# Attention and mixture of experts on one core: the first round's rows gathered in parts, two groups in quarter rows, one weight load in 4 KB pieces, fewer filler matmuls

## Chip, core and metric

The kernel runs on one core of one Trainium2 chip. The metric is device time in microseconds (us). The time before is the median of three runs; every time in this part comes from those runs or from the hardware profiler's record of one more execution.

Engines are named as in the profile: PE is TensorE (PEld its weight loads), DVE is VectorE, ACT is ScalarE, POOL is GpSimd, SP is SyncE, which here only starts DMA transfers. `L247` is line 247 of the kernel before. Where rows of the changed kernel are shown, the line numbers are those of the changed file.

## What is computed

```
attn = softmax(q k^T / 8) v                  # 8 batches x 8 heads, chunks of 64 tokens, head size 64
x    = attn as 4608 rows of 512              # fp32
logits = x @ w_gate                          # 8 experts
expert_idx = argmax(logits); gate_w = softmax(logits)[expert_idx]
for e in range(8):
    tok = rows whose expert is e; if more than capacity (80): keep the 80 with the largest gate_w
    h = relu(x[tok] @ w1[e])                 # 512 -> 1024
    out[tok] = gate_w[tok] * (h @ w2[e])     # 1024 -> 512; all other rows are zero
```

All weights and activations of the experts are fp32. One expert's `w1` or `w2` is 2 MB.

## The kernel before

**Up to the selection.** Attention runs over 36 tiles of 128 rows; its output rows go to a DRAM scratch tensor `xs`, from which rows are gathered later. Gating and the search for each expert's cut-off run beside it. Then the tokens that can be kept are packed: one-hot matrices `pk`, made on DVE in five compares (L849) and on ACT in three pairs of Abs and Relu (L859, L860), are multiplied on PE (L1100) into 128 candidates, and their keys stand in `kc` (L1112).

**Selection.** Every expert has 96 slots. For each expert PE turns its key column into a row (L1139), DVE counts how many candidates are larger (`rank`, L1120) and compares the rank with the slot numbers (`select`, L1126), which gives a 0/1 matrix `sel`. `place` (L166) multiplies `sel` with the candidates' row numbers and gate values. Slots are handled in groups of 32: expert e owns groups 3e to 3e+2, and round r works on groups 4r to 4r+3, so there are six rounds. Round 0 holds three groups of expert 0 and one of expert 1. `place` writes round 0 into `pl0` and rounds 1 to 5 into `pl1`; a DVE sum (L170) turns these into row numbers `gi0` and `gi1`.

**Gathers.** POOL starts an indirect DMA (L204) that fetches the 128 rows of a round from `xs` into `xg`, one row of 2 KB per partition. For rounds 0 and 1 PE turns `xg` by four transposes into PSUM (L217) and ACT copies the result to `xT` (L219), round 0 in two halves. Rounds 2 to 5 are fetched instead as four quarter gathers of 512 B per partition (L228, the addresses `giq` come from two DVE operations behind a spreading matmul L1163), so that DVE can turn them in blocks of 32 (L237).

**Experts.** `layer1(r, f)` (L247) handles two groups (j = 0, 1) with 16 PE products each, every product two passes in the trace; ACT applies ReLU (L252), DVE turns the result (L254). `layer2` (L264) follows one round later, DVE scales (L269), POOL scatters (L273). PE's order is: layer1 of round 0 and 1, layer2 of round 0, layer1 of round 2, layer2 of round 1, and so on.

**What sets the order.** The program is written out by hand: every engine runs its instructions in the order of the code, and waits are put in from the data that the instructions share. Weights come on SP's queue in the order of the code (`part`, called from `ahead`); expert 3's `w1` is held back by a POOL memset into its first column that stands behind the second gather (L1202), experts 4's `w1` and 3's `w2` by DVE copies that read the second gather's rows (L1204). `keep_warm(n)` (L871) puts n matmuls of 256 columns, whose result nobody reads, into PE's order. `RUN` makes a weight load move 16 KB at a time.

## Time and profile before

| what | value |
|---|---|
| median of 3 runs | 233.46 us (232.95 to 233.56) |
| the profiled execution, its own time | 233.38 us |
| its span, first to last instruction | 231.6 us |
| PE busy in the span | 217.0 us (94%) |
| DVE, ACT, POOL busy | 133.5, 73.0, 66.7 us |
| DMA | 84.81 MB, mean 366 GB/s |

The profiled execution's time is the span and what lies around it. "Busy" adds up the times in which an engine has an instruction running; matmuls are pipelined, so that a busy PE may also be doing fillers.

### The profile page before, as it was taken

How to read it: one execution, taken by the hardware profiler on the slowest of the kernel's cores; microseconds unless marked ns; L12 is line 12 of the kernel's file. 1: busy time of each engine (PE TensorE's matmuls, PEld its weight loads, DVE VectorE, ACT ScalarE, POOL GpSimd, SP SyncE). 2: the span in 40 equal slices, each digit the busy share in tenths (PEclk: the TensorE clock that was granted, in tenths of full speed). 3: DMA queues.
4: the chain of work that ended last, by engine and by line, in shares of the span. 5: the costliest groups of instructions: out<-in, count | busy, mean ns of one | idle time of the engine just before them, and what ended most of it. 6: DMA issues, size and time to landing. Idle time of an engine off the chain costs nothing. (4 is left out here: it accounts for less than half of the span.)

```text
span 231.6 us, 8390 instructions
## 1 busy us (share of the span) xinstructions
PE 217.0 (94%) x3604; PEld 143.0 (62%) x3604; DVE 133.5 (58%) x422; ACT 73.0 (32%) x159; POOL 66.7 (29%) x142
## 2 busy tenths in 40 slices
PE   7878999999898999999999999999999999999970
PEld 5667787877777787878776876653534436354220
DVE  6678687878779799878878866213231321302110
ACT  2124433333535635566585501210110201111000
POOL 8001203030303019292624427107033060411101
PEclk9999999999999999999999999999999999999998
DMA  6999999999999999998999977999999999998011
GB/s 214 362 409 396 413 410 417 421 421 420 416 419 408 372 406 402 410 413 284 379 420 420 417 298 279 333 423 427 431 405 428 441 397 425 444 420 362 5 44 38
DMA packets 16681, 84.81 MB, mean 366 GB/s; under 512 B 2752, under 2 KB 2880, under 8 KB 12288
## 3 DMA queue, kind: packets, MB, share of 16 engines
q1 hardware_dynamic: 12848, 71.84, 76.6%
q0 software_dynamic: 3648, 12.32, 13.7%
q8 instruction: 30, 0.49, 0.8%
q10 hardware_dynamic: 144, 0.07, 0.2%
q14 instruction: 11, 0.09, 0.1%
HBM read 64.03 MB, written 20.45 MB: 365 GB/s over the span
## 5 line engine op out<-in xcount | busy, mean ns | idle before, releaser
L247 PE MATMUL hc<-w,xtc 128*32 128x256 f32 x768 | 42.6, 379 | 0.3 <-ACT xtc L219 0.3
L264 PE MATMUL yc<-w,htc 128*32 128x512 f32 x384 | 42.1, 592 | 0.0
L419 PE MATMUL s<-kz,qv 128*64 128x128 f32 x544 | 37.2, 279 | 0.5 <-DMA qv<-in_qv 0.5
L247 PEld LDWEIGHTS hc<-w,xtc 128*32 128x32 f32 x768 | 24.8, 110 | 18.4 <-issue 2.4
L455 ACT ACTIVATE pT<-pt 128x512 f32<-128x512 f32 x36 | 21.4, 594 | 36.7 <-PE pt L453 36.5
L419 PEld LDWEIGHTS s<-kz,qv 128*64 128x64 f32 x544 | 29.0, 136 | 6.3 <-issue 6.1
L435 DVE TENSOR_REDUCE mx<-s 128x8 f32<-128x512 f32 (+1 forms) x37 | 24.9, 673 | 11.4 <-PE s L419 11.2
L264 PEld LDWEIGHTS yc<-w,htc 128*32 128x32 f32 x384 | 12.5, 110 | 26.6 <-issue 25.7
L478 PEld LDWEIGHTS o<-qv,pT 64*64 64x64 f32 x1120 | 19.8, 134 | 13.1 <-issue 9.6
L252 ACT ACTIVATE hsc<-hc 128x512 f32<-128x512 f32 x12 | 7.2, 598 | 62.6 <-PE hc L247 62.6
L478 PE MATMUL o<-qv,pT 64*64 64x65 f32 x1120 | 24.9, 224 | 2.1 <-DMA qv<-in_qv 1.2
L254 DVE STREAM_TRANSPOSE htc<-hsc 128x512 f32<-128x512 f32 x12 | 8.5, 711 | 31.1 <-ACT hsc L252 31.1
L437 DVE TENSOR_TENSOR sm<-s,mx 128x512 f32<-128x512 f32 (+1 forms) x37 | 24.7, 667 | 0.1
L497 DVE TENSOR_TENSOR x<-o,rc 128x512 f32<-128x512 f32 x35 | 24.1, 689 | 0.8
L453 PE MATMUL pt<-ct,sm 128*128 128x128 f32 x144 | 23.5, 285 | 0.2
L269 DVE TENSOR_SCALAR ysc<-yc,gatec 128x512 f32<-128x512 f32 x6 | 4.5, 750 | 33.1 <-PE yc L264 24.6
L513 PE MATMUL px<-ct,x 128*128 128x128 f32 x136 | 20.5, 273 | 0.0
L514 ACT COPY xT<-px 128x512 f32<-128x512 f32 x32 | 18.6, 580 | 0.0
L591 POOL TENSOR_TENSOR comp<-comp,ct 128x32 bf16<-128x32 bf16 x18 | 3.9, 234 | 50.3 <-DVE rc L492 40.8
L228 POOL DMA_INDIRECT xqc<-xs,giq x16 | 16.0, 1003 | 6.1 <-issue 4.8
L453 PEld LDWEIGHTS pt<-ct,sm 128*128 128x128 f32 x144 | 15.2, 140 | 2.8 <-DVE sm L437 0.4
L513 PEld LDWEIGHTS px<-ct,x 128*128 128x128 f32 x136 | 15.9, 141 | 0.8 <-issue 0.8
(223 smaller groups left out, 228.2 us busy)
## 6 DMA issues: line engine op xcount, KB each, us to landing
w<-in_w SPq DMA_DIRECT2D x12, 2048.0 KB, 22.6
qv<-in_qv SPq DMA_DIRECT2D x14, 1032.0 KB, 11.1
kz<-in_kh SPq DMA_DIRECT2D x34, 256.0 KB, 10.2
xs<-x POOLq DMA_DIRECT2D x8, 1024.0 KB, 11.7
w<-in_w SPq DMA_DIRECT2D x8, 1024.0 KB, 9.6
out<-zero SPq DMA_DIRECT2D x8, 1024.0 KB, 26.7
qv<-in_qv SPq DMA_DIRECT2D x2, 520.0 KB, 9.2
qv<-in_qv SPq DMA_DIRECT2D x2, 516.0 KB, 9.7
```

The source lines that it names most:

```text
L228: nc.gpsimd.indirect_dma_start(out=t[:, P * g:P * g + P], out_offset=None, in_=xs.rearrange("r (c d) -> (r c) d", c=4), in_offset=bass.Ind ...
L247: nc.tensor.matmul(h[32 * c:32 * c + 32, j, :], lhsT=xT[r][:, g, b, :], rhs=w[:, b, 256 * c:256 * c + 256], start=(b == 0), stop=(b == 3), ...
L264: nc.tensor.matmul(y[o:o + 32, :], lhsT=hT[r, g // 2][:, g % 2, c, :], rhs=getw(groups[r][g])[1][:, c, :], start=(c == 0), stop=(c == 7), ...
L419: nc.tensor.matmul(o, lhsT=a, rhs=b, start=True, stop=True)
L435: nc.vector.tensor_reduce(m8, s8, axis=AX.X, op=ALU.max)
L437: d['sub'] = lambda: nc.vector.tensor_tensor(d8, s8, to, op=ALU.subtract)
L453: nc.tensor.transpose(pt[:, pr, :], sv[:, pr, :], ident)
L455: nc.scalar.activation(pT, pt, AF.Exp, scale=0.125)
L478: nc.tensor.matmul(po[h][64 * u:64 * u + 64, 65 * pr:65 * pr + 65], lhsT=d['pT'][64 * h:64 * h + 64, pr, 64 * u:64 * u + 64], rhs=TT[T, r] ...
L497: nc.vector.tensor_tensor(x8, pov[..., 0:64], to, op=ALU.mult)
L513: nc.tensor.transpose(pm[:, pr, :], t['x'][:, r, P * pr:P * pr + P], ident)
L514: copy(t['xT'][:, :, P * r:P * r + P], pm)
```

## The change

It has six parts.

1. **Round 0 is gathered in parts.** The first 64 rows (groups 0 and 1, both of expert 0) are placed, summed and gathered (`xga`) as soon as expert 0's rank and `sel` are there. Groups 2 and 3 are fetched as two quarter gathers (`xgh`), whose addresses `gih` come from eight more `place` matmuls, a DVE sum and a DVE multiply-add.
2. **Turning.** `xga` is turned by four PE transposes of 64 columns that stand behind the `place` matmuls of rounds 1 to 5, ahead of the matmuls for the flag and the quarter addresses; `xgh` by one DVE transpose ahead of `targets`. Round 1's PE transposes move from between the two halves of round 0's layer 1 to the middle of its second half.
3. **Selects.** `sel` of experts 2, 3 and 5 is made on ACT (Abs, Relu) instead of DVE.
4. **Fillers.** `keep_warm` has 1 instead of 2 (three times), 2 instead of 4, 14 instead of 18, 4 instead of 6, none instead of 8.
5. **Expert 3's `w1`** moves 4 KB at a time instead of 16 KB, and waits for the last transpose of `xga` instead of the POOL memset.
6. The buffers of `xg` are 3 instead of 4; `xga` and `xgh` are set to zero early in the program.

```diff
+    xga = mp.tile([P, DM], F32, name="xga")
+    xta = mp.tile([P, 4, 64], F32, name="xta")
+    xgh = mp.tile([P, 2 * P], F32, name="xgh")
+    xth = mp.tile([P, 2, 4, 32], F32, name="xth")
...
-        def layer1(r, f):
+        def layer1(r, f, between=None):
             h = pp.tile([P, 2, 256], F32, name=f"h{tag}{r}_{f}", tag="h", bufs=4)
             for j in range(2):
+                if j and between:
+                    between()
...
-                            h[32 * c:32 * c + 32, j, :], lhsT=xT[r][:, g, b, :],
+                            h[32 * c:32 * c + 32, j, :],
+                            lhsT=xT[r][f][:, j, b, :] if extra and r == 0 else xT[r][:, g, b, :],
...
-        for r in range(NQ if extra else 2):
-            gather(r)
-            if extra and r == 1:
-                extra(-1, xg)
         if extra:
+            extra(-1, xg)
+            gather(1)
             quarters(2, None)
             extra(0, xg)
-        xpose(0)
+            xT[0] = xta.rearrange("p b (g t) -> p g b t", g=2), xth
...
-                layer1(r, 1)
+                layer1(r, 1, (lambda: xpose(1)) if extra and r == 0 else None)
...
                 if rt in (7, 33, 34):
-                    keep_warm(2)
+                    keep_warm(1)
...
+                ab = gk.tile([P, P], BF16, name=f"as{e}", tag="ab")[:, 0:SL]
+                nc.scalar.activation(ab, io_b[:, 0:SL], AF.Abs, bias=rk[:, e:e + 1], scale=-1.0)
+                nc.scalar.activation(sel[e], ab, AF.Relu, bias=1.0, scale=-1.0)
...
-            keep_warm(4)
-            for e in (0, 1):
-                rank(e)
-            for e in (0, 1):
-                select(e)
+            keep_warm(2)
+            first = ps2.tile([P, 3, 5], F32, name="pl0", tag="g")
+            pl0 = first[:, 0:1]
+            ph = first[:, 1:3, 0:2]
...
+            rank(0)
+            select(0)
+            rank(1)
+            place_first((0, 1))
+            with nc.allow_low_precision(reason="row numbers are whole and far below 2^24"):
+                nc.vector.tensor_reduce(gi0[0:64], pl0[0:64, :, 0:2], axis=AX.X, op=ALU.add)
+            nc.gpsimd.indirect_dma_start(
+                out=xga[0:64], out_offset=None, in_=xs[:, :],
+                in_offset=bass.IndirectOffsetOnAxis(ap=gi0[0:64], axis=0),
+                bounds_check=NT * 512 - 1, oob_is_err=False)
+            select(1)
             rank(2)
-            pl0, gi0 = place(mp, ps2.tile([P, 1, 5], F32, name="pl0", tag="g"), sel_part, cb, "c", 0, 1)
-            keep_warm(18)
+            select(2, "a")
+            for g in (2, 3):
+                e, j = divmod(g, 3)
+                for o in range(0, P, 32):
+                    nc.tensor.matmul(ph[o:o + 32, g - 2], lhsT=sel_part(e, j),
+                                     rhs=cb[:, 0:2, e], start=True, stop=True,
+                                     tile_position=(0, o))
+            place_first((2, 3))
+            nc.vector.tensor_reduce(rh, ph, axis=AX.X, op=ALU.add)
+            with nc.allow_low_precision(reason="row numbers are whole and far below 2^24"):
+                nc.vector.tensor_scalar(gih, rh, 4.0, ct[:, C_Q:C_Q + 1], op0=ALU.mult,
+                                        op1=ALU.add)
+            for g in range(2):
+                nc.gpsimd.indirect_dma_start(
+                    out=xgh[:, P * g:P * g + P], out_offset=None,
+                    in_=xs.rearrange("r (c d) -> (r c) d", c=4),
...
+            keep_warm(14)
             for e in range(3, NE):
                 rank(e)
-                select(e - 1)
-            select(NE - 1)
+                select(e, "a" if e in (3, 5) else "v")
...
-            keep_warm(6)
+            keep_warm(4)
+            for b0 in (0, 2):
+                pm = sb[b0 // 2][:, 0:P].rearrange("p (b t) -> p b t", b=2)
+                for b in range(2):
+                    late = nc.tensor.transpose(
+                        pm[:, b, :], xga[0:64].rearrange("p (m b) -> p b m", b=4)[:, b0 + b],
+                        ident[0:64, 0:64])
+                nc.scalar.copy(xta[:, b0:b0 + 2], pm)
...
-            keep_warm(8)
...
+            nc.vector.transpose(xth, xgh.rearrange("p (g t b) -> p g b t", g=2, b=4))
             gate, sv = targets(mp, [(pl0, gi0), (pl1, gi1)], "c")
...
                 if r < 0:
-                    part(3, 0, True)
+                    tc.add_manual_dep(part(3, 0, None, 4096).ins, late.ins.name, mybir.DependencyInfo(
+                        mybir.DependencyClass.Sync, mybir.DependencyReason.DATA))
                     clear(3.5, nc.sync, 2)
```

How this stands on the engines is shown at three places, before and after. Rows name the line, the operation, out<-in and the size; a number behind a name only tells buffers apart, and "waits" names the engines or DMA lanes whose signal the instruction waits for.

On DVE, from the candidates' keys `kc` on, before:

```order
L1112 TENSOR_REDUCE kc<-s_110 128x8 [waits PE_49]
L1120 SCALAR_TENSOR_TENSOR bt_2711,rk<-kr_2697,kc,ct 128x128 [waits PE_49]
L1120 SCALAR_TENSOR_TENSOR bt_2713,rk<-acc,kc,ct 128x128 [waits PE_49]
L1126 TENSOR_SCALAR sel_2715<-io_b,rk 128x96 [waits DVE_49]
L1126 TENSOR_SCALAR sel_2717<-io_b,rk 128x96 [waits DVE_49]
L1120 SCALAR_TENSOR_TENSOR bt_2719,rk<-kr_2700,kc,ct 128x128 [waits PE_49]
L170 TENSOR_REDUCE gic_2726<-pl_2721 128x1 [waits PE_49]
```

And after:

```order
L1123 TENSOR_REDUCE kc<-s_114 128x8 [waits PE_49]
L1131 SCALAR_TENSOR_TENSOR bt_2716,rk<-kr_2700,kc,ct 128x128 [waits PE_49]
L1138 TENSOR_SCALAR sel_2718<-io_b,rk 128x96 [waits DVE_49]
L1131 SCALAR_TENSOR_TENSOR bt_2720,rk<-acc,kc,ct 128x128 [waits PE_49]
L1175 TENSOR_REDUCE gic_2713<-pl_2712 64x1 [waits PE_49]
L1138 TENSOR_SCALAR sel_2728<-io_b,rk 128x96 [waits DVE_49]
L1131 SCALAR_TENSOR_TENSOR bt_2730,rk<-kr_2703,kc,ct 128x128
L1190 TENSOR_REDUCE rh<-pl_2712 128x2 [waits PE_49]
L1192 TENSOR_SCALAR gich<-rh,ct 128x2 [waits DVE_49]
L1131 SCALAR_TENSOR_TENSOR bt_2768,rk<-kr_2703,kc,ct 128x128
```

The first sum of row numbers now stands behind two ranks and one select instead of three ranks and two selects, and DVE waits for PE once more, at `rh`.

On POOL, from the last instruction ahead of the gathers on, before:

```order
L1108 COPY seen<-pk_2640 128x1
L204 DMA xgc_2868<-xs,gic_2726 128x512
L204 DMA xgc_2872<-xs,gic_2788 128x512
L1202 MEMSET w_3_2876 128x1
L228 DMA xqc_2880<-xs,giq 128x128 x4
```

And after:

```order
L1119 COPY seen<-pk_2646 128x1
L1176 DMA xga<-xs,gic_2713 64x512
L1195 DMA xgh<-xs,gich 128x128 x2
L208 DMA xgc_2892<-xs,gic_2812 128x512
L232 DMA xqc_2896<-xs,giq 128x128 x4
```

Two more indirect DMAs now stand ahead of round 1's gather, and the memset is gone.

On PE, round 0's transposes and layer 1, before (`xpc` is the transposes' PSUM tile, `hc` that of layer 1):

```order
L217 MATMUL xpc_0_2900<-ct,xgc_2868 128x128 x2
L217 MATMUL xpc_2_2904<-ct,xgc_2868 128x128 x2
L247 MATMUL hc_0_2908<-w_0_487,xtc_2899 32x256 x32
L217 MATMUL xpc_0_2946<-ct,xgc_2872 128x128 x4
L247 MATMUL hc_1_2952<-w_0_487,xtc_2899 32x256 x16
L247 MATMUL hc_1_2952<-w_1_1871,xtc_2899 32x256 x16
```

And after (the rows left out are the small matmuls for the flag and the quarter addresses, L1219 and L1222):

```order
L1213 MATMUL s_113<-ct,xga 128x64 x2
L1213 MATMUL s_114<-ct,xga 128x64 x2
...
L253 MATMUL hc_0_2915<-w_0_493,xta 32x256 x32
L253 MATMUL hc_1_2952<-w_0_493,xth 32x256 x16
L221 MATMUL xpc_0_2970<-ct,xgc_2892 128x128 x4
L253 MATMUL hc_1_2952<-w_1_1877,xth 32x256 x16
```

The first half of layer 1 reads `xta`, the second `xth`, and round 1's transposes stand 16 products later than before.

## Rows read from the trace of the kernel before

**Rows 1.** The page's first line.

```profile
span 231.6 us, 8390 instructions
```

**Rows 2.** Busy time by stretch: from:to, length, busy (x instructions), PEclk, DMA share, GB/s.

```profile
135.00:141.00 6.00, 5.61 (x75) 4.45 (x76) 4.82 (x38) 0.66 (x3) 2.57 (x4) 1.00 0.53 182
141.00:224.00 83.00, 83.00 (x1155) 37.73 (x1156) 19.10 (x34) 7.92 (x14) 21.29 (x24) 1.00 0.89 365
224.00:229.00 5.00, 0.60 (x8) 0.00 (x0) 0.75 (x1) 0.00 (x0) 0.98 (x1) 1.00 0.13 44
```

**Rows 3.** Timeline of PE: start us, us, line, operation, tile, count.

```profile
133.06 0.71 PE L1100 MATMUL s<-comp,pk 128*128 128x40 bf16 x10
...
134.97 0.60 PE L871 MATMUL pwarm<-io_b,ones_b 128*128 128x256 bf16 x4
135.50 0.19 PE L166 MATMUL pl<-cb,sel 128*32 128x5 bf16 x4
...
138.24 0.19 PE L166 MATMUL acc<-cb,sel 128*32 128x5 bf16 x3
138.36 0.83 PE L871 MATMUL pwarm<-io_b,ones_b 128*128 128x256 bf16 x6
...
140.03 0.65 PE L217 MATMUL xpc<-ct,xgc 128*128 128x128 f32 x4
140.94 3.66 PE L247 MATMUL hc<-w,xtc 128*32 128x256 f32 x64 [0.26 <-ACT xtc L219]
```

**Rows 4.** Timeline of DVE in the selection.

```profile
130.18 2.94 DVE L849 TENSOR_TENSOR pk<-io_h,ptok_b 128x1024 bf16<-128x1024 bf16 x5
...
134.41 0.35 DVE L1120 SCALAR_TENSOR_TENSOR bt<-kr,kc,ct 128x128 bf16<-128x128 f32 x1 [0.42 <-PE kr L1139]
...
134.68 0.35 DVE L1120 SCALAR_TENSOR_TENSOR bt<-acc,kc,ct 128x128 bf16<-128x128 f32 x1
...
134.95 0.40 DVE L1126 TENSOR_SCALAR sel<-io_b,rk 128x96 bf16<-128x96 bf16 x2
...
135.74 0.16 DVE L170 TENSOR_REDUCE gic<-pl 128x1 int32<-128x2 f32 x1
...
138.47 0.17 DVE L170 TENSOR_REDUCE gic<-acc 128x5 int32<-128x10 f32 x1 [0.29 <-PE acc L166]
```

**Rows 5.** Timeline of POOL: the indirect DMAs' issue.

```profile
136.19 1.15 POOL L204 DMA_INDIRECT xgc<-xs,gic  x1 [3.50 <-DVE bt L1120]
138.92 1.00 POOL L204 DMA_INDIRECT xgc<-xs,gic  x1 [1.58 <-DVE gic L170]
...
140.71 1.00 POOL L228 DMA_INDIRECT xqc<-xs,giq  x1 [0.67 <-DVE gatec L182]
142.01 1.00 POOL L228 DMA_INDIRECT xqc<-xs,giq  x1 [0.31 <-issue]
```

**Rows 6.** Tile xgc: from issue to landing of the two row gathers.

```profile
DMA to landing us min/median/max: 3.6/3.6/3.7
```

**Rows 7.** Tile xqc: the block transposes, and issue to landing of 16 quarter gathers.

```profile
L237 DVE STREAM_TRANSPOSE xtc<-xqc x4: 1116/1116/1661, 157.1 to 198.4; 128x512 f32<-128x512 f32 x4
...
DMA to landing us min/median/max: 5.9/6.5/8.2
```

**Rows 8.** DMA queues in 138 to 139.5 us: packets, MB, share of 16 engines.

```profile
q0 software_dynamic: 80, 0.26, 52.3%
```

**Rows 9.** Timeline of ACT: the first copy out of round 0's transposes.

```profile
140.51 0.37 ACT L219 COPY xtc<-xpc 128x256 f32<-128x256 f32 x1 [1.66 <-PE xpc L217]
```

**Rows 10.** Expert 6's w2: SP's issue, KB and us to landing, first PE use.

```profile
177.92 6.42 SPq L117 DMA_DIRECT2D w<-in_w  x1
...
w<-in_w SPq DMA_DIRECT2D x1, 2048.0 KB, 31.5
...
210.68 0.61 PE L264 MATMUL yc<-w,htc 128*32 128x512 f32 x4
```

**Rows 11.** SP's issue of expert 3's w1.

```profile
140.06 0.33 SPq L113 DMA_DIRECT2D w<-in_w  x1
```

More of the change, by code (lines that the diff above doesn't have):

```diff
@@ L278, in scatter @@
                 tc.add_to_no_dep_group("rows", put.ins)
-        for r in range(NQ if extra else 2):
-            gather(r)
-            if extra and r == 1:
-                extra(-1, xg)
         if extra:
+            extra(-1, xg)
+            gather(1)
             quarters(2, None)
             extra(0, xg)
-        xpose(0)
+            xT[0] = xta.rearrange("p b (g t) -> p g b t", g=2), xth
+        else:
+            gather(0)
+            gather(1)
+            xpose(0)
         for r in range(NR + 1):
@@ L290, in experts @@
                 layer1(r, 0)
-            if r + 1 < (NQ if extra else NR):
+            if r + 1 < NR and not extra:
                 xpose(r + 1)
             if r < NR:
-                layer1(r, 1)
+                layer1(r, 1, (lambda: xpose(1)) if extra and r == 0 else None)
             if extra and NQ <= r + 1 < NR:
@@ L1122, in rank, with select @@
                     op0=ALU.subtract, op1=ALU.is_gt, accum_out=rk[:, e:e + 1])
-            def select(e):
+            def select(e, way="v"):
                 sel[e] = gk.tile([P, SL], BF16, name=f"sel{e}", tag=f"sel{e}", bufs=1)
-                nc.vector.tensor_scalar(sel[e], io_b[:, 0:SL], rk[:, e:e + 1], None,
-                                        op0=ALU.is_equal)
+                if way == "v":
+                    nc.vector.tensor_scalar(sel[e], io_b[:, 0:SL], rk[:, e:e + 1], None,
+                                            op0=ALU.is_equal)
+                    return
+                ab = gk.tile([P, P], BF16, name=f"as{e}", tag="ab")[:, 0:SL]
+                nc.scalar.activation(ab, io_b[:, 0:SL], AF.Abs, bias=rk[:, e:e + 1], scale=-1.0)
+                nc.scalar.activation(sel[e], ab, AF.Relu, bias=1.0, scale=-1.0)
             def sel_part(e, j):
@@ new lines, in attention_moe, with place_first @@
+            ph = first[:, 1:3, 0:2]
+            gi0 = mp.tile([P, 1], I32, name="gic0")
+            gih = mp.tile([P, 2], I32, name="gich")
+            rh = gk.tile([P, 2], F32, name="rh", tag="rh", bufs=1)
+            def place_first(groups):
+                for g in groups:
+                    e, j = divmod(g, 3)
+                    nc.tensor.matmul(pl0[32 * g:32 * g + 32, 0], lhsT=sel_part(e, j),
+                                     rhs=cb[:, :, e], start=True, stop=True,
+                                     tile_position=(0, 32 * g))
@@ new lines, in attention_moe @@
+            with nc.allow_low_precision(reason="row numbers are whole and far below 2^24"):
[5 more added lines that the diff above has]
+                    in_=xs.rearrange("r (c d) -> (r c) d", c=4),
+                    in_offset=bass.IndirectOffsetOnAxis(ap=gih[:, g:g + 1], axis=0),
+                    bounds_check=NT * 2048 - 1, oob_is_err=False)
@@ L1192, in attention_moe, with part @@
                                                  reuse_waits="tile"))
-            def part(e, l, after=None):
+            def part(e, l, after=None, run=RUN):
                 w = weights.setdefault(e, [None, None])
@@ L1200, in part @@
                 if after is not None:
-                    if after is True:
-                        nc.gpsimd.memset(w[l][:, 0, 0:1], 0.0)
-                    else:
-                        nc.vector.tensor_copy(w[l][:, 0, 0:1], after)
-                fetch(w[l], e, l, 0, a)
+                    nc.vector.tensor_copy(w[l][:, 0, 0:1], after)
+                return fetch(w[l], e, l, 0, a, run)
             def ahead(r, xg):
                 if r < 0:
-                    part(3, 0, True)
+                    tc.add_manual_dep(part(3, 0, None, 4096).ins, late.ins.name, mybir.DependencyInfo(
+                        mybir.DependencyClass.Sync, mybir.DependencyReason.DATA))
                     clear(3.5, nc.sync, 2)
@@ L1222, in attention_moe @@
             clear(2, nc.sync)
-            experts(ep, pp, lambda r: gi1[:, r - 1:r] if r else gi0, si, gate, weights.get, "c",
+            experts(ep, pp, lambda r: gi1[:, r - 1:r], si, gate, weights.get, "c",
                     ahead, lambda g: giq[:, g % 4, g // 4 - NQ:g // 4 - NQ + 1])
```

17 lines of the change are left out of this document (10 added, 7 removed).

## Prediction

> **What bounds the kernel now.** I read three views in this order. The table by stretch says what the end hangs on: from 141 to 224 us PE is busy 83.00 of 83.00 us at a granted clock of 1.00, so 2.4 GHz [rows 2]. PE therefore waits for nothing behind the first layer-1 matmul, which starts at 140.94 [rows 3], and what follows it is a fixed 231.6 - 140.94 = 90.66 us [rows 1, 3] as long as every operand stays in time. Whatever moves that first matmul moves the end by as much.
>
> The timelines of PE, DVE and POOL then give the chain that ends at 140.94, read backwards: the first copy out of the transposes 140.51 + 0.37 [rows 9]; the transposes, matmuls from 140.03 [rows 3]; the rows' landing, 3.6 us behind the issue at 136.19 [rows 5, 6], so 139.8; the sum of row numbers at 135.74 [rows 4]; `place` at 135.50, behind four fillers from 134.97 [rows 3]; rank and select from 134.41 [rows 4]; the last candidate matmuls, 133.06 + 0.71 [rows 3].
>
> Third, the issue and landing of transfers: which of them has slack when PE comes earlier. This execution took 233.38 us, 1.78 more than its span and 0.08 less than the median of 233.46. My sum is made against 233.38.
>
> **The change, step by step.** (a) Three fillers less among the candidate matmuls. A filler takes (0.83 - 0.28)/5, about 0.11 us, of PE (six are 0.83 us [rows 3], and the last is not shortened by a successor). The last compare on DVE ends at 130.18 + 2.94 = 133.12 [rows 4], and the last four of the ten matmuls that begin at 133.06 start near 133.35. So the keys can come at most about 0.2 earlier. Bounds 0 and 0.2; I take 0.16.
>
> (b) The first index. Rank 0 starts at 134.41 - 0.16 = 134.25 and its `sel`, which now stands right behind it, is ready at about 134.25 + 0.35 + 0.04 + 0.24 = 134.88 (two selects take 0.40 [rows 4], one of them alone some 0.24). PE is the later one: `place` started 0.53 us behind four fillers [rows 3], two fewer give 0.22, and with (a) `place` comes at 135.50 - 0.38 = 135.12, the sum at 135.36, POOL's issue at 136.19 - 0.38 = 135.81. ACT's selects and experts 1 and 2 lie behind this and don't touch it.
>
> (c) The landing. 3.6 us is the price for 128 rows. No row shows 64. Above: the same 3.6, so 139.4. Below: half of POOL's 1.15 us and half of the transfer. 80 packets filled 52.3% of 1.5 us [rows 8], so 0.78 us, and half is 0.39. That gives 3.6 - 0.57 - 0.39 = 2.6, so 138.4. I take 3.3, hence 139.1, since POOL's 1.00 us is the same for rows of 2 KB and of 512 B [rows 5], which looks like a cost per instruction or per row and leaves me undecided between those.
>
> (d) When PE is ready for the transposes. DVE's ranks 3 to 7 now stand behind `rh` and `gih`. `place` for groups 2 and 3 must wait for the second select (135.36 + 0.08 + 0.24 = 135.68), `rh` follows at about 136.0, `gih` at 136.2, rank 3 at 136.35; from there five ranks 0.27 apart (134.41 to 134.68 [rows 4]), two selects of 0.16, three waits of some 0.12 for a rank's result and the last select's 0.24 make 2.27, so 138.62. `place` follows a select by 0.05: its last three matmuls, now at 138.24 [rows 3], come at 138.65, and four fillers later it is 139.1. So PE is ready at 139.1, together with the landing. Rows that landed sooner would gain nothing.
>
> (e) From transposes to layer 1. Now 140.94 - 139.92 = 1.02 us, the weight load of the first transpose being 0.11 ahead of its matmul at 140.03. The new ones move 64 columns instead of 128 and the copy has 128 instead of 256, so it costs between 0.19 and 0.37 [rows 9]; I take 0.85. **Layer 1 starts at 139.1 + 0.85 = 139.95; say 140.0, against 140.94: 0.94 us earlier** (bounds 0.6 and 1.0).
>
> (f) What has to be in time behind it. Half a round of layer 1 takes 3.66 us [rows 3]. *Groups 2 and 3* are needed at 140.0 + 3.6 = 143.6. POOL issues indirect DMAs 1.30 apart [rows 5], so the second quarter gather starts at 135.81 + 2.6 = 138.4; with 3.6 to landing and half of a 1.12 us transpose [rows 7] `xth` stands at 142.6, one us ahead. *Round 1's rows* are needed in the middle of the second half, at 140.0 + 3.6 + 1.8 = 145.4. Their index comes at 138.47 + 0.4, but POOL is free only at 139.7; landing 3.6 later is 143.3, 2.1 ahead. Beside a weight stream the quarter gathers took 5.9 to 8.2 [rows 7], which would be 145.6 to 147.9. Expert 3's weights, issued at 140.06 [rows 11] and now near 139.85, start to flow just when this gather does. I take 4.7, so 144.4, in time.
>
> The Trainium skill, "DMA: Bandwidth & Descriptors", section "Queues, rings and completion order", says that each DMA engine serves its queues in turn, a packet at a time. By it a gather behind 4 KB packets waits less than one behind 16 KB packets, round 1's rows land near 143.6, and the sum stays as it is; by the quarter gathers' median of 6.5 it would lose 0.8 us. No run here shows a gather beside weights in 4 KB pieces.
>
> (g) The weights. PE gains on a DMA stream that runs without a gap. Expert 6's `w2` lands at 177.92 + 31.5 = 209.4 and is needed at 210.68 [rows 10]: 1.26 us of slack, the least that I found. 0.94 leaves 0.32. Round 1's gather, 0.78 us of all engines, moves from a gap into the stream, in which expert 3's load begins 0.2 sooner: the stream is 0.4 later. So about 0.1 us of the gain is lost there.
>
> (h) The rest costs nothing. DVE's block transpose holds back `targets`, but the scale factors are first read after layer 2 of round 0, and two rounds of layer 1, four times 3.66 us [rows 3], stand before that. The two weight loads behind `targets` come later too, onto a queue that still holds expert 3's load. The memsets run early on POOL, which idles there.
>
> **Sum:** 0.94 - 0.1 = 0.85 us less, 233.38 - 0.85 = 232.53; against the median of 233.46 I say 232.55. Bounds of this case: 0.55 (233.0) to 1.1 (232.3).
>
> **Rivals.** *Slower, round 1's rows.* If the gather of round 1, now third behind two others on POOL, lands after 145.4, PE stands in the middle of layer 1. It decides from a landing of 5.7 us on; the whole gain is gone at 6.6, and at 8.2 PE waits 2.5, so 233.38 - 0.94 + 2.5 = 234.9. For it: the 5.9 to 8.2 of rows 7. Against: those stood behind 16 KB pieces already flowing. *No change.* The stream of weights, not PE, sets the last rounds: if it comes 0.8 later instead of 0.4, the gain is 0.45, and if 64 rows land no faster than 128 and the keys come no earlier, 0.4: 232.95. For it: both slacks are a third of a us. *The clock.* Nineteen fillers go. If the granted clock fell to 1.2 GHz as layer 1 starts, half a round would cost 3.66 us more, 236.2. Against it: from 224 to 229 us PE was busy 0.60 of 5.00 us and the clock was still 1.00 [rows 2], and no gap that I expect is over 1 us.
>
> The Trainium skill, "TensorE: Matmul & The Clock Gate", section "Why this matters for your kernels", tells to keep gaps between bursts short, since an idle PE is set back to half clock. By that rule the missing fillers speak against the change, and the time would be the 236.2 of the rival; the trace agrees with it only after the last matmul.
>
> **How the numbers follow.** 0.3% or 0.70 us is about what a measurement of this kernel can tell from no change. The forecast has 0.60, of which a fifth is a gain under 0.70 us; no change 0.20; round 1's rows late 0.12, of which a third stays within 0.70; the clock 0.04; 0.04 for a loss that I don't see. So faster 0.48, same 0.12 + 0.20 + 0.04 = 0.36, slower 0.08 + 0.04 + 0.04 = 0.16. I predict 232.55 us. The range reaches from 232.1, below the best of the forecast's bounds, to 233.9, into the case of late rows, and leaves out its worse part and the clock; the forecast's own is 232.3 to 233.0.
>
> **What would show it.** The first indirect issue near 135.8 and its landing near 139.1; layer 1 from 140.0; no wait in PE for `xth` (143.6), for round 1's rows (145.4) or for a weight (209.7); clock 1.00 throughout; the last matmul near 223.1. Wrong would be made of: PE idle between 143 and 148, a granted clock under 1.00 past 139, or a PE wait for a DMA after 200.

## The result and the profile after

| | before | after |
|---|---|---|
| median | 233.51 us (4 runs, 232.95 to 233.66) | 236.82 us (4 runs, 235.7 to 237.64) |
| profiled execution / its span | 233.38 / 231.6 us | 237.23 / 235.4 us |

The change made the kernel slower: 1.0128 times before, 95% interval 1.009 to 1.0167. The forecast was 232.55 us. Ratios leave out executions more than 1.5% slower than the fastest of the same kernel; medians keep them.

The busy time by stretch of the changed kernel (from:to, length, busy of PE, PEld, DVE, ACT, POOL, granted clock, DMA share, GB/s) answers to [rows 2]:

```profile
141.00:146.00 5.00, 5.00 (x95) 3.08 (x97) 3.82 (x24) 1.03 (x3) 3.78 (x5) 1.00 0.81 265
146.00:150.00 4.00, 1.34 (x18) 0.69 (x8) 1.04 (x6) 0.00 (x0) 1.39 (x2) 0.98 1.00 314
150.00:154.00 4.00, 4.00 (x45) 1.94 (x48) 0.24 (x1) 0.95 (x2) 0.00 (x0) 0.59 1.08 432
154.00:228.00 74.00, 74.00 (x1008) 30.12 (x1004) 15.69 (x20) 6.21 (x11) 17.62 (x20) 1.00 0.86 353
```

Two stretches are new. From 146 to 150 PE works 1.34 of 4 us, and from 150 to 154 it works all the time, but at a granted clock of 0.59; the trace has it at 0.5, which is 1.2 GHz, for 3.41 us. Before, nothing stood between 141 and 224. PE's timeline, to set beside [rows 3], names the wait:

```profile
139.24 0.61 PE L880 MATMUL pwarm<-io_b,ones_b 128*128 128x256 bf16 x4
140.44 0.69 PE L1213 MATMUL s<-ct,xga 64*128 64x64 f32 x4 [0.59 <-DMA xga<-xs,gic]
...
141.27 3.66 PE L253 MATMUL hc<-w,xta 128*32 128x256 f32 x64
144.75 1.91 PE L253 MATMUL hc<-w,xth 128*32 128x256 f32 x32
149.32 0.80 PE L221 MATMUL xpc<-ct,xgc 128*128 128x128 f32 x4 [2.66 <-DMA xgc<-xs,gic]
150.04 3.51 PE L253 MATMUL hc<-w,xth 128*32 128x256 f32 x32
...
215.38 13.91 PE L271 MATMUL yc<-w,htc 128*32 128x512 f32 x128
```

PE stands 2.66 us in the middle of layer 1's second half, before the transposes of round 1's rows (`xgc`), and the 32 matmuls behind them take 3.51 us where the 32 ahead took 1.91: the lower clock. In the trace of before the last layer-2 row is "210.68 13.92", so it ended at 224.60; here it ends at 215.38 + 13.91 = 229.29, 4.69 later. That is the later start of layer 1 (141.27 for 140.94 [rows 3], 0.33), the wait (2.66) and half of 3.41 us of clock (1.70): 4.69. Behind the last matmul this execution needs 0.8 to 0.9 us less, so the span grows by 3.8.

The timeline of the issuing queues (POOL, and SP as SPq) tells where both delays come from; it answers to [rows 5, 11]:

```profile
120.75 0.54 POOL L509 DMA_DIRECT2D xs<-x  x1 [0.49 <-DVE x L506]
...
137.45 1.06 POOL L1176 DMA_INDIRECT xga<-xs,gic  x1 [4.29 <-DVE bt L1131]
138.82 1.05 POOL L1195 DMA_INDIRECT xgh<-xs,gich  x1 [0.30 <-DVE bt L1131]
140.17 1.00 POOL L1195 DMA_INDIRECT xgh<-xs,gich  x1 [0.31 <-issue]
...
141.16 0.39 SPq L113 DMA_DIRECT2D w<-in_w  x1
...
141.47 1.00 POOL L208 DMA_INDIRECT xgc<-xs,gic  x1 [0.30 <-issue]
```

The tile `xgc` has its landing, as in [rows 6]:

```profile
DMA to landing us min/median/max: 7.8/7.8/7.8
```

And the table of DMA issues, for the store of 120.75 alone, has its size and its time to landing:

```profile
xs<-x POOLq DMA_DIRECT2D x1, 256.0 KB, 15.6
```

Round 1's gather goes out at 141.47, 0.3 us behind expert 3's first weights (SP, 141.16), and lands 7.8 us later instead of 3.6 or 3.7. And the first gather goes out at 137.45 although its row numbers were summed at 135.83. The row names a DVE instruction that had long been done; what ended last is the last store to `xs`, issued at 120.75 and landed 15.6 us later, at 136.35. POOL must wait for it, since the rows are read from `xs`.

### The profile page after: what moved, and what is told of

Its sections match the earlier page's. It is cut to its first block, busy times and chain, and to the rows that moved or that the text cites. A ratio compares the mean times of both kernels' runs of the same rounds, so it can differ in the third digit from the quotient of the medians.

```text
span 235.4 us, 8375 instructions
## 1 busy us (share of the span) xinstructions
PE 218.3 (93%) x3593; PEld 140.0 (59%) x3593; DVE 134.0 (57%) x422; ACT 74.9 (32%) x165; POOL 69.4 (29%) x145
## 5 line engine op out<-in xcount | busy, mean ns | idle before, releaser
L253 PE MATMUL hc<-w,xtc 128*32 128x256 f32 x640 | 35.4, 379 | 0.0
L253 PEld LDWEIGHTS hc<-w,xtc 128*32 128x32 f32 x640 | 19.3, 110 | 17.2 <-issue 2.7
L271 PEld LDWEIGHTS yc<-w,htc 128*32 128x32 f32 x384 | 11.5, 110 | 27.5 <-issue 26.6
L261 DVE STREAM_TRANSPOSE htc<-hsc 128x512 f32<-128x512 f32 x12 | 8.5, 711 | 31.2 <-ACT hsc L259 31.2
```

The source lines that it names most:

```text
L253: nc.tensor.matmul(h[32 * c:32 * c + 32, j, :], lhsT=xT[r][f][:, j, b, :] if extra and r == 0 else xT[r][:, g, b, :], rhs=w[:, b, 256 * c: ...
L271: nc.tensor.matmul(y[o:o + 32, :], lhsT=hT[r, g // 2][:, g % 2, c, :], rhs=getw(groups[r][g])[1][:, c, :], start=(c == 0), stop=(c == 7), ...
```

## The experiments

| run | median | before, same chip | ratio (95%) |
|---|---|---|---|
| e1_hold_w3 | 238.32 | 236.06 | 1.0122 (1.0047 to 1.0196) |
| e2_16k_pieces | 237.30 | 236.06 | 1.0060 (1.003 to 1.0089) |
| e3_fewer_fillers_alone | 235.84 | 236.06 | 1.0001 (0.9972 to 1.0031) |
| e4_fillers_back | 239.13 | 236.06 | 1.0107 (1.006 to 1.0154) |
| e5_before_again | 235.31 | 235.85 | one run |
| e6_after_again | 237.68 | 235.85 | 1.0054 (1.002 to 1.0087) |
| e7_late_quarters | 237.55 | 235.85 | 1.0042 (0.9997 to 1.0087) |
| e8_hold_late_quarters | 235.85 | 235.85 | 0.9976 (0.9934 to 1.0018) |
| e9_pairs | 233.91 | 233.90 | 1.0003 (0.9965 to 1.004) |
| e10_w2_4k | 233.77 | 233.90 | 0.9988 (0.9951 to 1.0024) |
| e11_more_fillers | 233.60 | 233.90 | 0.9974 (0.9937 to 1.001) |
| e12_before_w_first | 239.17 | 233.90 | 1.0217 (1.0168 to 1.0266) |
| e13_early_clear | 237.19 | 236.00 | 1.0048 (1.0014 to 1.0083) |
| e14_before_early_clear | 236.87 | 236.00 | 1.0022 (0.9991 to 1.0054) |
| e15_early_clear_row | 238.42 | 236.00 | 1.0080 (1.005 to 1.0111) |
| e16_before_pairs | 234.42 | 236.00 | 0.9916 (0.9883 to 0.9949) |
| e17_pairs_w2_4k | 235.35 | 236.24 | 0.9955 (0.9927 to 0.9983) |
| e18_before_pairs_w2_4k | 233.84 | 236.24 | 0.9884 (0.9836 to 0.9932) |

The kernel before took 233.5 us in the first runs and 233.9 on the chip of e9 to e12, but 235.9 to 236.2 on the three other chips (e1 to e4, e5 to e8, e13 to e18), so each ratio stands against before on its own chip. The second group below tells most of why.

### Round 1's rows and the weights

**e1**: the changed kernel, expert 3's `w1` held behind round 1's gather.

```diff
-            extra(-1, xg)
             gather(1)
+            extra(-1, xg)
...
-                    tc.add_manual_dep(part(3, 0, None, 4096).ins, late.ins.name, ...)
+                    part(3, 0, True, 4096)     # behind a POOL memset
```

> The changed kernel, with expert 3's w1 held back again by a memset on POOL that stands behind the gather of round 1 (still in 4 KB pieces). Theory A (round 1's rows are late because that load flows when they are asked for): they land 3.6 to 4 us after their issue instead of 7.8, PE's wait of 2.7 us in the middle of layer 1 and the half clock behind it go, and the time is 232.5 to 233.7. Theory B (the 4 KB pieces slow the gather): the pieces are the same but start later, so the landing is again 3.6 to 4; told apart from A by the next run. Theory C (it is late because two quarter gathers stand ahead of it on POOL): landing stays near 7.8 and the time near 236.

**e2**: the changed kernel with 16 KB pieces again (`part(3, 0, None)`).

> The changed kernel, expert 3's w1 in 16 KB pieces as before, its release as changed. Theory A: round 1's rows land as late or later, 7 to 9 us after issue, time 236 to 238. Theory B: they land 4 to 5.5 us after issue and the time is 233 to 234.

**e12**: the kernel before with nothing but the order of two issues turned round.

```diff
         for r in range(NQ if extra else 2):
-            gather(r)
             if extra and r == 1:
                 extra(-1, xg)
+            gather(r)
```

> The kernel before, with nothing of the change in it but the order of two issues: the fourth expert's first weights are released ahead of round 1's gather (issue at about 137.6) and not behind it. Theory A: the gather lands 7 to 9 us after its issue at 139 instead of 3.0 to 3.7, 146 to 148 where the transposes want it at 144.5 to 146.7; TensorE waits 1 to 3 us in the middle of layer 1, partly in place of the slow issue; time 0.5 to 2 us above before, ratio 1.002 to 1.009. Rival (the late landing needs the changed kernel's other gathers in the queue): it lands in under 5 us and the time is that of before or better, since the weights start 2.5 us sooner.

e12 reproduces the loss in the kernel before. PE's timeline:

```profile
141.12 3.66 PE L247 MATMUL hc<-w,xtc 128*32 128x256 f32 x64 [0.26 <-ACT xtc L219]
148.88 0.72 PE L217 MATMUL xpc<-ct,xgc 128*128 128x128 f32 x4 [4.10 <-DMA xgc<-xs,gic]
```

The gather's landing, and the table by stretch behind the wait:

```profile
DMA to landing us min/median/max: 9.6/9.6/9.6
```

```profile
150.00:154.00 4.00, 4.00 (x48) 2.13 (x44) 0.00 (x0) 0.22 (x1) 0.00 (x0) 0.58 0.93 348
```

Same wait, 4.10 us now, same clock behind it, and 2.2% more time. Over all traces the order alone sorts the landing of round 1's rows: behind the weights 7.8 (after), 7.9, 8.0 and 8.1 us in 4 KB pieces (e4, e6, e7), 9.1 and 9.6 in 16 KB pieces (e2, e12); ahead of them 3.4 to 3.8 (e8 to e11, e13, e15), 4.6 (e1) and 5.0 (e17). So the pieces are worth 1.0 to 1.8 us of landing time and the order 3 to 6.

A late landing costs time only where PE gets to the transposes before it. That is so in the changed kernel's trace above and in e12. In e2, e4, e6 and e7 the rows land as late, but PE comes later still. In e6, the changed kernel on another chip, they land at 149.14 and the transposes start at 150.53 without a wait, so e6's expectation of one failed, and its ratio of 1.0054 lies under the forecast of 1.006 to 1.017. What holds PE back there is the subject of the next part. And e1, whose rows came in 4.55 us, was not faster than the changed kernel. The order was a cause, not the only one.

### TensorE's slow issue

e1's PE waits for no DMA in layer 1. It waits for nothing at all (its timeline, "issue" being time without a wait that the profile shows):

```profile
141.34 3.09 PE L253 MATMUL hc<-w,xta 128*32 128x256 f32 x47
144.74 1.38 PE L253 MATMUL hc<-w,xta 128*32 128x256 f32 x5 [0.31 <-issue]
146.96 0.38 PE L253 MATMUL hc<-w,xta 128*32 128x256 f32 x1 [0.84 <-issue]
147.67 0.38 PE L253 MATMUL hc<-w,xta 128*32 128x256 f32 x1 [0.34 <-issue]
148.37 0.83 PE L253 MATMUL hc<-w,xta 128*32 128x256 f32 x9 [0.33 <-issue]
148.86 0.41 PE L253 MATMUL hc<-w,xth 128*32 128x256 f32 x3
149.04 0.38 PE L253 MATMUL hc<-w,xta 128*32 128x256 f32 x1
```

Sixty-four matmuls on `xta` that take 3.66 us elsewhere end at 149.42, 8.08 us after their start. From about 143.7 on they are issued in ones and twos, most steps 0.45 to 0.7 us apart and some 1.2, at a granted clock of 1.00. Layer 1 up to round 1's transposes takes 9.74 us here (141.34 to 151.08) and 5.32 in e9 below, which has no slow issue: 4.4 us lost.

**e5, e6**: the kernel before and the changed kernel, unchanged, on one chip.

> The kernel before, unchanged, once more with its trace, since three of the four runs so far (the ones with the clock at 1.00) show a thing that the first trace of before does not: in the middle of expert 0's first layer TensorE issues its matmuls one by one, some 0.7 us apart, with no wait that the profile names (143.7 to 148.3 us with the fourth expert's weights held, 143.6 to 148 with 16 KB pieces, 143.6 to 146.1 in the kernel before with fewer fillers), and all of those ran beside a kernel before of 236.06 us instead of 233.5. If the slow issue belongs to the chip or to the run, it stands in this trace too, about 2 to 2.5 us long, and the first layer ends some 2.5 us later against its start than in the first trace (last matmul 86.2 us after the start of layer 1, not 83.7). If it belongs to the fillers that were taken out, this trace has none and 83.7 us.

> The changed kernel, unchanged, on the same chip as the others of this call. Theory (round 1's rows come late behind the fourth expert's weights): round 1's gather lands 7 to 9 us after its issue, TensorE waits in the middle of layer 1 and the ratio to before is 1.006 to 1.017, as in the first runs. Rival (the 1.013 is a matter of the first chip): ratio within 0.997 to 1.003.

**e7, e8**: round 2's four quarter gathers behind the first half of layer 1, in the changed kernel and in e1.

```diff
-            quarters(2, None)
...
                 layer1(r, 0)
+                if extra and r == 0:
+                    quarters(2, hs[0])
```

> The changed kernel with the four quarter gathers of round 2 issued after the first half of expert 0's layer 1 (paced on ScalarE's relu of it) and not right behind round 1's gather. Theory P: TensorE's slow issue comes from GpSimd's indirect DMAs; in the three traces that have it, it ends 1.9 us after the last quarter gather's issue. Then layer 1's first half runs in 3.7 us without a gap and any slow issue stands after 145.5. Theory W: it comes from the weights that begin to flow at 141 to 143; then it stands at 143.6 as before. Theory I: it is the place in TensorE's code; then it stands some 47 to 58 matmuls into layer 1 as before. For round 1's rows: if the four gathers behind it hold its rows back, it lands in under 5 us; if the weights ahead of it do, in 7 to 9 us as in the changed kernel, with the wait at the same place.

> As the run before this, with the fourth expert's first weights held behind round 1's gather as well (which landed in 4.55 us that way). Theory A (order of gather and weights decides the wait) with P (the quarter gathers make the slow issue): neither the wait for round 1's rows nor the slow issue is left in layer 1, last matmul 83.7 to 84.5 us after the start of layer 1, and the time comes to 0.995 to 1.000 of before or less. With W or I the slow issue stays, 88 us, ratio 1.01 as with the weights alone held.

The kernel before has it as well on that chip (e5: 64 matmuls from 141.11 to 147.19, 6.08 us). The timeline of e5, PE and POOL's first and last quarter gather:

```profile
140.89 1.00 POOL L228 DMA_INDIRECT xqc<-xs,giq  x1 [0.67 <-DVE gatec L182]
141.11 5.11 PE L247 MATMUL hc<-w,xtc 128*32 128x256 f32 x59 [0.26 <-ACT xtc L219]
...
144.80 1.00 POOL L228 DMA_INDIRECT xqc<-xs,giq  x1 [0.30 <-issue]
...
146.55 0.64 PE L247 MATMUL hc<-w,xtc 128*32 128x256 f32 x5 [0.34 <-issue]
```

The last slow step ends 1.75 us after the last of the row of gathers went out. In e1, e2, e3, e6 and e15 that number is 1.97, 2.0, 1.87, 1.87 and 1.86; in e7 and e8, where the row stands 7 us later and PE some 100 matmuls further on, the slow stretch moves with it (in e8 it ends at 155.22, the last issue was 153.47: 1.75). So it is neither the weights (W) nor the place in the code (I), but the row of gathers (P). e8, which differs from e7 in the order alone, is 1.7 us faster in the medians. The wait that this saves is not shown by e7's trace: its clock is at 0.5 for 6.8 us from 140.77, and PE gets to the transposes at 149.90, behind the rows (149.63). e8's profiled execution took 238.3 us, 2.4 above its median, with the clock at 0.5 for 6.8 us; of PE's times in it only the place of the slow stretch is used.

This also tells what e6 lost. From the start of layer 1 to round 1's transposes it needs 9.20 us where e5, on the same chip, needs 6.01: a longer slow issue, with 3.4 us at 1.2 GHz in it.

At half clock the slow issue does not show. e14 below has the row of gathers too (issued from 141.45 to 145.35), on a chip whose other traces slow down beside one, but PE is at a granted clock of 0.5 from 142.87 to 149.70:

```profile
144.84 6.03 PE L247 MATMUL hc<-w,xtc 128*32 128x256 f32 x64
```

The lower clock alone would make 6.09 of the usual 3.66 us (half of the 4.86 us from 144.84 to 149.70 is lost). In e4 the slow stretch starts at 147.10, 1.65 us after the clock is back at 1.00.

**e9 and e16**: the row cut into two pairs, 4 us apart, in e8 and in the kernel before.

```diff
+                if extra and r == 0:
+                    quarters(2, hs[0], 0, 2)     # after layer1(0, 0)
...
+                if extra and r == 0:
+                    quarters(2, hs[0], 2, 4)     # after layer1(0, 1)
```

> As e8 (round 1's rows ahead of the weights, round 2's quarters late), with the four quarter gathers in two pairs: two after the first half of expert 0's layer 1, two after the second. In the traces so far TensorE's slow issue begins 2.4 to 3.0 us after the first of a row of gathers that GpSimd issues back to back and ends 1.7 to 2.0 us after the last. Theory P1 (it takes a long row of them): a pair is 1.3 us long, so none or nearly none is left, 2 to 2.3 us less than e8, ratio 0.987 to 0.994. Rival P2 (each gather brings its share): two slow stretches, of 1 us or so each, ratio as e8 (0.994 to 1.002).

> The kernel before with round 2's quarter gathers in two pairs, after the halves of expert 0's layer 1, and nothing else changed. P1: where before has the slow issue (spans of 233 to 235 us) it loses it, ratio 0.990 to 0.996, and its times spread less; where the chip shows none, 0.998 to 1.002. P2 (each gather brings its share): 0.998 to 1.002 on either.

e9 missed: level with before, not below. But its chip shows no slow issue in any of four traces, three of them with four gathers in a row (e10, e11, e12), so it could tell nothing of pairs. e16, on a chip that shows it, could: its timeline, PE and POOL's four gathers.

```profile
142.81 3.66 PE L248 MATMUL hc<-w,xtc 128*32 128x256 f32 x64 [0.26 <-ACT xtc L219]
...
147.08 11.14 PE L248 MATMUL hc<-w,xtc 128*32 128x256 f32 x192
...
147.91 1.02 POOL L230 DMA_INDIRECT xqc<-xs,giq  x1 [0.53 <-DVE htc L255]
149.24 1.00 POOL L230 DMA_INDIRECT xqc<-xs,giq  x1 [0.30 <-issue]
...
152.46 1.02 POOL L230 DMA_INDIRECT xqc<-xs,giq  x1 [0.53 <-issue]
153.78 1.00 POOL L230 DMA_INDIRECT xqc<-xs,giq  x1 [0.30 <-issue]
```

No "issue" gap is left and the time falls by 0.84%. A little is: the 192 matmuls take 11.14 us, where in the trace of before they take 10.57:

```profile
145.21 10.57 PE L247 MATMUL hc<-w,xtc 128*32 128x256 f32 x192
```

Over layer 1 of rounds 0 and 1 the pairs leave 0.3 to 0.6 us in e16 to e18. e16 also moves the gathers to a later place, so it does not part the pairs from the move. e13 and e15 below do, since on the same chip they differ in nothing but the pairs: e15 has the slow issue (its last row "155.96 2.40 ... [0.81 <-issue]"), e13 none, 1.2 us apart. P1 stands; P2, two stretches of 1 us and no gain, falls.

### Fillers and clock

**e3**: the kernel before with the change's smaller `keep_warm` numbers. **e4**: the changed kernel with the old ones. **e11**: e8 with 13 fillers more.

```diff
-            keep_warm(14)
+            keep_warm(18)
...
-            keep_warm(4)
+            keep_warm(8)
...
+            keep_warm(5)
             pq = acc[:, 1, 0:8 * (NR - NQ)]...
```

> The kernel before with the change's fewer fillers alone (1, 2, 14, 4 and none). Theory A (the clock fell because PE stood waiting for the rows): granted clock stays 1.00 to the end of the last matmul, time 232.9 to 233.5, since some fillers lay on the path. Theory D (the clock fell for want of fillers): a stretch of half clock past 139 and 1 to 2 us more than before.

> The changed kernel with the fillers of before (2, 4, 18, 6 and 8). Theory A: PE still waits about 2.7 us for round 1's rows and the clock still falls after it, time 236 to 237.5. Theory D: the clock stays at 1.00 and the time is 1.5 us under the changed kernel, 235 to 235.5.

> As e8, with 13 fillers more: four in the wait for the second batch of positions, four ahead of the turning of the first 64 rows, five between it and the sums for the quarters. Theory C (the clock falls at 140 to 142 where TensorE idled between 138 and 141): no fall in the trace, granted clock 0.994 or more in nine of ten runs (e8 had three below 0.991, the second run of the changed kernel eight of ten), time 0 to 1.5 us below e8, the less the fewer falls e8 has. Rival: the fall comes all the same, as it did with the old fillers back, and the time is that of e8 or up to 0.5 more for fillers that stand in the way.

e3 is level with before, and its trace shows no fall of the clock; but 4 of its 10 runs have a mean clock under 0.99, none of the 19 of before on that chip. e4's clock falls with the old fillers back, for 3.4 us from 142.0, and PE has no wait for rows there, so both of its forecasts missed. Of e11's twelve runs two had a mean clock under 0.991, of e10's ten on the same chip three; its forecast, a mean clock of 0.994 or more in nine of ten runs, failed: 5 of 12 had it. In the median the missing fillers cost nothing; whether they let the clock fall in single executions stays open.

### The stores and the first gather

**e10**: e8 with expert 2's weights, which flow while `xs` is stored, in 4 KB pieces.

```diff
-            part(2, 0)
-            part(2, 1)
+            part(2, 0, None, 4096)
+            part(2, 1, None, 4096)
```

> As e8, with expert 2's weights, which flow while the rows are stored to xs, in 4 KB pieces and not 16 KB. Theory S: the first gather goes out when the last store of xs has landed (136.54 there in e8, issue 137.64; 135.04 and 136.27 in e1; 134.63 and 136.35 in the second run of the changed kernel), and stores share the rings with the weights packet by packet: the last store then lands 1 to 4 us earlier, the first gather's issue falls to about 135.8 to 136.2, which its index sets, and its rows land at 138.7 to 139.1. Rival: the stores land as before (133.5 to 136.5) since the rings are merely full, and the issue stays at 136.3 to 137.6; or they land earlier and the issue doesn't move, which would clear the stores.

The last store of e10 in the table of DMA issues:

```profile
xs<-x POOLq DMA_DIRECT2D x1, 256.0 KB, 8.3
```

And its timeline, the sum of the first row numbers and POOL's first gather:

```profile
135.20 0.15 DVE L1176 TENSOR_REDUCE gic<-pl 64x1 int32<-64x2 f32 x1 [0.19 <-PE pl L1168]
...
135.64 1.07 POOL L1177 DMA_INDIRECT xga<-xs,gic  x1 [3.10 <-DVE sel L1139]
```

The store lands in 8.3 us instead of 13.5 (e9), and the gather goes out 0.44 behind its sum. It does so in e9 too, whose store landed at 133.89. Where the store is late the gather follows it by 1.10: after 136.35 and 137.45, e8 136.54 and 137.64, e11 136.13 and 137.22. So the issue is the later of sum + 0.44 and store + 1.10, and in the changed kernel's trace the store cost 137.45 - (135.83 + 0.44) = 1.18 us. The landing of that store is a matter of the execution (133.8 to 137.2 over all traces with 16 KB pieces).

### Where the gain goes at the end

In e9 and e10 everything on the path of the prediction is as forecast: layer 1 starts at 140.24 and 140.18, no wait in it, no slow issue. Their time is that of before. The timeline of e9, SP's first weights and then the end:

```profile
141.05 0.39 SPq L113 DMA_DIRECT2D w<-in_w  x1
...
201.06 1.02 POOL L281 DMA_INDIRECT out<-ysc,si  x1 [11.93 <-SPq L1289]
...
210.27 0.75 DVE L277 TENSOR_SCALAR ysc<-yc,gatec 128x512 f32<-128x512 f32 x1 [11.42 <-DMA out<-ysc,si]
...
211.07 13.94 PE L272 MATMUL yc<-w,htc 128*32 128x512 f32 x128 [0.67 <-DVE ysc L277]
```

Read from the bottom: PE waits 0.67 us for a PSUM buffer that DVE has to empty, DVE for an SBUF buffer (`ys`) whose scatter has to land, the scatter at 201.06 for the last clear of `out`. In the trace that clear lands at 200.13 (198.69 in before, where the scatter goes out at 199.61). The transfers run without a gap from expert 3's `w1` to this clear, and `w1` now stands behind two gathers more: 141.05, not 140.06 [rows 11].

The weights themselves were as late. Expert 7's `w1` landed at 204.98, and PE's weight loads waited for it:

```profile
205.02 4.91 PEld L254 LDWEIGHTS hc<-w,xtc 128*32 128x32 f32 x96 [0.51 <-SPq L1289]
```

Expert 6's `w2`, issued at 179.71, landed 31.2 us later, at 210.89; PE's layer 1 had ended at 210.41. Without the scatter PE would still have waited until 210.89, 0.48 of its 0.67 us.

**e13, e15**: e9 and e8 with e10's pieces, and one clear moved into the gap ahead of 141. **e14**: the kernel before with that clear moved.

```diff
-CLEARS = {1: (1, 4, 5), 2: (6, 7, 8)}
+CLEARS = {1: (4, 5), 2: (6, 7, 8)}
...
             clear(2, nc.sync)
+            clear(1, nc.sync)
```

> The changed kernel with round 1's rows ahead of the weights, round 2's quarter gathers in pairs, expert 2's weights in 4 KB pieces, and the clear of rows 512 to 1023 of the output moved from behind expert 5's weights to the idle stretch ahead of 141. Theory E (the end was held by the last clear, through the scatter and the buffer of round 0's results): that clear is out of the later row of transfers, which ends 2 to 2.6 us sooner; the first scatter goes out at about 198 instead of 201.06, TensorE doesn't wait at 210, last matmul 83.7 us after the start of layer 1; the first rows land up to 1 us later beside the clear (3.1 to 4.1 us after issue). Sum: 0 to 0.7 us less than the kernel with pairs, ratio to before 0.994 to 1.000. Rival: the clear delays the first 64 rows and round 1's by more than it frees at the end, ratio 1.000 to 1.006.

> The control: the kernel before with that clear moved alone. Theory E: TensorE has no wait at 210 in before, so nothing is gained at the end; its gathers land 0 to 1 us later beside the clear and their rows are waited for, ratio 1.000 to 1.005. Rival (an earlier end of the transfers is worth time by itself): 0.99 to 0.998.

> As the first, with round 2's four quarter gathers back to back and not in pairs. If the slow issue needs a long row of gathers (P1) and this chip shows it, this one has 2 us of it at some 148 to 151 and the first has none: 1 to 2 us apart. If the chip shows none, the two are level within 0.5 us.

The rival was right. e13's first rows landed 6.2 us after their issue (142.41, where the clear itself landed at 142.58), and the clock fell behind the wait:

```profile
142.45 0.75 PE L1217 MATMUL s<-ct,xga 64*128 64x64 f32 x4 [2.63 <-DMA xga<-xs,gic]
143.13 0.19 PE L1223 MATMUL ptot<-inc,ones_b 128*128 128x8 bf16 x1
143.18 0.25 PE L1226 MATMUL acc<-parts,spread 128*128 128x8 bf16 x4
143.35 4.92 PE L254 MATMUL hc<-w,xta 128*32 128x256 f32 x64
```

PE had no wait at 210 any more, as the theory wants, but PE was also 2.6 us late. That the end gave the gain back rests on e9's and e17's rows, not on a version without it, and by e9's rows moving the clear alone could have given back no more than 0.2 us.

### What is left of the change

**e17**: the changed kernel with order, pairs and 4 KB pieces for expert 2 (e9 and e10 together). **e18**: the kernel before with pairs and these pieces (e16 and e10's edit).

> The changed kernel with round 1's rows ahead of the weights, round 2's quarter gathers in pairs, and expert 2's weights in 4 KB pieces. Theory E: layer 1 starts 0.7 us sooner than in the next run, and the end gives it back in the wait for round 0's results buffer at some 210, since the row of transfers that the last clear and the scatters hang on starts 0 to 1 us later; level with the next run within 0.7 us, ratio to before 0.988 to 0.998. Rival (the gain comes through): 0.7 us or more below the next run.

> The kernel before with pairs, and expert 2's weights in 4 KB pieces. The first gather goes out at 2.4 us after the token list (index bound) and not after the last store, which landed at 137.18 in the kernel before with pairs: 0 to 1.5 us less than that kernel where the stores are late, ratio to before 0.986 to 0.994. Rival: the stores matter only in the profiled execution, ratio 0.990 to 0.996 as with pairs alone.

e18 has the lowest ratio of the study, though its interval overlaps that of e16, so what the 4 KB pieces add to the pairs is not clear of noise. The change costs 1.5 us on top of it. e18's layer 1 starts at 141.71 and its last matmul ends at 225.82; e17's at 140.86 and 225.68. Of 0.85 us 0.14 is left. In e17's trace the last layer 1 and the wait for the `ys` buffer (DVE waits 10.6 us for its scatter) take 7.54 us where e18's take 6.91, and the layer 1 from 176.16 takes 7.40, with an "issue" gap at 177.5, 2.2 us after the last gather of round 4. The two come to more than the 0.71 us lost, since e18 too needs 0.45 us more than before from layer 1 to the last matmul.

The profiled executions are 0.96 us apart: 0.62 lies outside the span (2.4 us in e17 and e13, 2.0 in e9, and 1.8 to 1.9 elsewhere), 0.48 behind the last matmul (6.47 against 5.99), less the 0.14. The other 0.55 us of the medians goes with the clock: 6 of e17's 12 runs have a mean clock under 0.99, none of e18's 6. Why the span is surrounded by more time in the changed kernel with pairs no run shows. e17's forecast, level with e18 within 0.7 us or 0.7 below it, missed both ways.

## Why the prediction was wrong, step by step

**(f) failed.** Its words were "I take 4.7, so 144.4, in time", for an issue at 139.7. The gather went out at 141.47 and took 7.8 us. Even from 139.7 it would have landed at 147.5, 2.1 us after the 145.4 of the step. [rows 7] had the right price, 5.9 to 8.2 us beside weights; I set it aside because those gathers stood behind 16 KB pieces that already flowed. e1 and e12 show that the order of the two issues decides. The rival "round 1's rows" came true with 2.66 us of wait (2.5 forecast for a landing of 8.2).

The rule of "DMA: Bandwidth & Descriptors" in the Trainium skill, section "Queues, rings and completion order", that an engine serves its queues in turn a packet at a time, spoke for a price below 5.9 us behind small pieces. Its sign agrees with e2 and e12 (1.0 to 1.8 us between the pieces), and the stores of e10 bear it out well (13.5 to 8.3 us). For the gather, issued behind the weights, it was no ground to go below 5.9.

**(b) half failed.** The sum of the row numbers came 1.10 us behind the first rank (135.83 - 134.73) instead of 1.33 [rows 4], 0.23 sooner where I had 0.22. But POOL's issue hangs on the last store as well, which I never listed; it cost 1.18 us here, more than the whole forecast gain, and e10 takes it away.

**The clock** was a rival for another place. "No gap that I expect is over 1 us" fell with (f): the 2.66 us gap was followed by 3.41 us at 1.2 GHz, 1.70 us lost. In all five traces with a PE gap of 2.37 to 4.10 us at 139 to 149 the clock fell (after, e12 to e15). The page "TensorE: Matmul & The Clock Gate" of the Trainium skill, section "Why this matters for your kernels", asks for short gaps between bursts, and these five agree. The four falls in e4, e6, e7 and e8 go beyond it: PE had no gap over 1.16 us there, and what set them off is open.

**(a), (c), (d), (e) held.** (a): the first rank of the changed kernel stands 0.32 later than before in an execution whose stores are 0.45 later, so 0.13 earlier for 0.16. (c): 64 rows landed in 2.94 us (bounds 2.6 to 3.6; 3.3 taken), 2.8 to 3.7 in the other kernels where no clear lay in the way. (d): PE is done with what stands ahead of the transposes 5.12 us after the first rank (139.85 against 134.73; the step had 4.85) and waits for the rows, as the step said. (e): 0.83 us from the first transpose to layer 1, as said 0.85. In e10, with the store out of the way, layer 1 starts at 140.18 where I had 140.0. Groups 2 and 3 of step (f) were in time (`xth` at 143.61, needed at 144.75).

**(g) was too small.** 0.1 us was to be lost to the stream of weights. It can be judged in e9 alone, where PE came as early as planned. There expert 6's `w2`, the transfer that the step names, landed at 210.89, 0.48 us after PE was ready for it, and the scatter behind the last clear, which the step does not name, made it 0.67, nearly all of what layer 1 had gained. The mechanism, a stream without a gap that starts later, was right; its cost was about six times mine.

**Not foreseen at all**: the slow issue. It costs before 2.4 us in e5 and the changed kernel, which puts two gathers more ahead of round 2's on POOL's queue, up to 4.4 (e1). The first trace of before has none.

## What to carry to other kernels

A transfer that a busy engine will wait for must be issued ahead of the next big load, whatever the size of that load's pieces: here the order was worth 3 to 6 us of the gather's landing, and a gain of 0.9 us was planned across it. Before an index is made earlier, list everything that its DMA waits for, the writes to the tensor that it reads too, and follow a gain to the last use of every buffer behind it, not only to the weights. And pace rows of indirect DMAs beside dense matmuls; pairs 4 us apart cost 0.3 to 0.6 us, and four in a row 2.4 or more on three of the four chips of the experiments.

## What the hardware showed that I had not expected

TensorE issues matmuls in ones and twos, most steps 0.45 to 0.7 us apart, at full clock and with no wait in the profile, from 2.5 to 3.2 us after GpSimd starts a row of back-to-back indirect gathers until 1.7 to 2.0 us after the last one. It was seen on three of the four chips of the experiments, and not in the first trace of before. That of after shows none up to its wait for rows (32 matmuls from 144.75 ran in 1.91 us, though round 1's gather had gone out in a row at 141.47), and the wait hides what would come later. PE's own pace seems to matter: at half clock it did not show (e14), and beside the quarter gathers of rounds 3 to 5, which run mostly beside layer 2, where PE issues half as many instructions, next to nothing is lost. Why is open. A 64-row gather issued while a 1 MB clear is still in the rings lands with the clear (142.41 and 142.58 in e13).
